# A planner's order table and its landing allowances replaced in a windowed-attention and expert-attention kernel

## The chip, the cores and the metric

One core of a Trainium2 chip runs the whole program. The metric is the device time of one execution in microseconds (us); the figure that counts is the median of several runs. TensorE is called PE here, VectorE DVE, ScalarE ACT, GpSimd POOL, and SP is the queue of SyncE, which issues nearly all DMAs.

## What is computed

Eight batches of 576 positions go through two layers. The first is attention in a window of 64 positions with 8 heads of 64; the second is four causal attentions ("experts"), of which a gate picks the best two for each position.

```python
# layer 1, for each batch and head
scores = scale * q @ k.T                      # 576 x 576, only 0 <= i - j < 64 is kept
attn = softmax(where(mask, scores, -1e9))
x = concat_heads(attn @ v)                    # 576 x 512
# layer 2, for each batch
logits = x @ w_gate                           # 4 experts, the best 2 are kept, softmax of the two
for e in range(4):
    q, k, v = x @ wq[e], x @ wk[e], x @ wv[e] # 576 x 64 each
    a = softmax(causal(scale * q @ k.T))
    out += weight_of_e * (a @ v @ wo[e])      # zero where e is not among the best two
```

## The kernel before

The code does not issue its instructions as it comes to them. `Plan` records them as operations (a run of matmuls that belongs together is one operation, everything else is one instruction), works out what depends on what, and then issues all of them in an order that it finds by playing the program through with its own costs. Four things set that order: the string `ORDER`, which gives PE's blocks one letter each and is obeyed strictly; due times on the other engines, worked back from the place that a block has in `ORDER` (`deadlines`); the table `EARLY`, which shifts the due time of single operations; and the costs that `Plan` assumes, one of which is `op["land"]` in `Plan.add`, the time from the end of a transfer's data to the moment when its reader may start. On the chip each engine then works its list off strictly from the top.

The letters of `ORDER`: s, t and a are layer 1 in 36 units of eight blocks of 64 positions: s the scores, t the transposes of the softmax, a the product with v. K, k, Q, q, V and W are the projections of layer 2 (k and q the second halves of a batch, W the last block of two batches), 1, 3, 2, 4 and 0 the score blocks of one *half*, A and B its products with v, O and o the output projection. A half is one batch and one pair of experts, so there are 16 of them, numbered 0 to 15 here. z is a pair of matmuls on the identity matrix whose result nobody reads; there are six. T and U are transposes on PE, in the last two halves only.

In halves 0 to 13 the probabilities are transposed without PE (`s2_t`): after the last score block, 4, the softmax is finished on DVE, ACT and POOL, DVE transposes 32x32 blocks into the buffer `ST` (`st` in the rows), and 16 DMAs on SP's queue move them to the buffer `PT2` (`pt`). These are the late moves inside SBUF that the title of the change speaks of; they are called the 16 moves below. `PT2` exists once: the 16 moves of a half wait for A and B of the half before. A and B both read all of it.

On the same queue of SP, in order, go the loads of layer 1 (`q`, `k` of 288 KB and `v` of 576 KB for each of 32 pairs of heads) and the stores of the result (`out`). Each of q, k and v has three buffers, so a load waits for the last s or a block that reads the buffer; a store waits for ACT's or DVE's copy out of PSUM. An instruction of SP that waits holds all behind it.

The weights come in f32 and are split by `split_weights` into two f32r parts (`wkhi`, `wklo` and so on); the result of layer 1 is split in the same way into `xh` (a copy on ACT) and `xl` (a subtraction on DVE) by `s1_av`. A projection block multiplies, for each of four pairs of heads in turn, xh, xl and xh again.

Of the kernel before, what the change touches and what calls it, by code (L numbers as in the profile page):

```python
# [31 lines left out]
OLATE = 1.7  # L32
TTAG = 1
ORDER = (
    "sszzsztstazazstKKVtssQaatQsVtastkqaatzss1tV2aaVt0s3s4WVqtVVkqQ132aV4s0tKQKtksaAa"
    "B132qta40kQtKsssAaBOO1324tqOV0VOtkKaaBAsstV132a0VQtkqaABass41tVWVOVOKOtqssa3240t"
    "OKOQkaBAatVk13240qtQQsssBaAaVtVOV13240VtOQsstOOqKqaBaAatKk13240qtkssaBAWVOVtOOQs"
    "s13240VKVtOOkaaAB1324tKQk0qssaaABtOO13s24tOO0KQktqBaAa13240VtVqVVaaABOWKOOQk1324"
    "0KOVqOQVBAVkKV13240QkqBAT1TOT23T4U0TUOTUOUTUOTAUBUooUoUoUoABOOOOO"
)  # L40
EARLY = {
# [52 lines left out]
}  # L94
HOLD = 13000.0
TAIL = 2
SHORT = 0
WARM = 6
TPE = 99
BPOS = 0.05  # L100
SJOIN = 1
PARTS = ((0, 5), (5, 9))
# [4 lines left out]
class Plan:  # L107
# [17 lines left out]
    def add(self, engine, call, name, out, args, kw):  # L125
        if engine == "P" and self.run is not None and self.run["engine"] == "P":
            op = self.run
# [7 lines left out]
        outs = [x for x in (out, kw.get("accum_out")) if x is not None]  # L135
# [8 lines left out]
                row = inner[0].nbytes() / inner[0].shape[0] / (inner[0].shape[1] if len(inner[0].shape) == 4 else 1)  # L144
                rows = inner[0].nbytes() / row
                op["transfer"] = outs[0].nbytes() / 420 + rows * (1.2 if row < 2048 else 0.4)
            op["land"] = 1650 if len(inner) == 2 else 2300 if outs[0].space == bass.MemoryType.SB else 500
        sb = [x for x in outs + ins if x.space != PSUM]
        op["port"] = engine == "G" or engine == "V" and (
            len([x for x in sb if x in ins]) > 1 or len(sb) == len(outs + ins) and name in (  # L150
# [1015 lines left out]
```

## Time and profile before

| | us |
|---|---|
| median of 3 runs | 424.93 (424.13 to 425.73) |
| the profiled execution | 423.19 |
| its span, first to last instruction | 421.5 |

| engine | busy, us | share of the span |
|---|---|---|
| PE | 404.1 | 96% |
| PE's weight loads | 364.4 | 86% |
| DVE | 310.3 | 74% |
| POOL | 276.2 | 66% |
| ACT | 269.6 | 64% |

The page's share of busy time for PE counts every matmul until its result has drained, so that neighbours overlap; what a block really takes is read from the start of one block to the start of the next, in the timeline. A row of the timeline gives the start from the beginning of the span, the length, engine and line, the operation, output and inputs, the shape, how many are merged, and in brackets an idle time ahead of it with what ended it. All recorded instructions carry one source line, so operations are told apart by their tiles.

### The profile page before, as it was taken

The page shows a single profiled execution, that of the slowest core. Times are in us where ns is not written, and L with a number is a line of the kernel's source. Part 1 is how long each engine was busy: PE and PEld are TensorE (multiplying, and loading weights), DVE is VectorE, ACT ScalarE, POOL GpSimd, SP SyncE. Part 2 cuts the span into 40 slices and gives each one's busy share as a digit, 9 for nine tenths or more (in the row PEclk, how much of TensorE's full clock was granted, in tenths as well). Part 3 has the DMA queues.
Part 4 walks back from the last instruction along what each step waited for, and adds up shares of the span by engine and source line. Part 5 has one row for each costly group of instructions (what it writes and reads, how often), then busy time and mean ns, then how long its engine had stood idle before and what let it go on. Part 6 is the DMA issues. An engine that isn't in the chain of part 4 may idle for free. (4 is left out here: it accounts for less than half of the span.)

```text
span 421.5 us, 13748 instructions
## 1 busy us (share of the span) xinstructions
PE 404.1 (96%) x5168; PEld 364.4 (86%) x5168; DVE 310.3 (74%) x997; ACT 269.6 (64%) x854; POOL 276.2 (66%) x473
## 2 busy tenths in 40 slices
PE   5799999999999999999699999999899999999995
PEld 4688989999899989899598998998889999998874
DVE  4899997879876876768677878679696756456722
ACT  3676685767685858566558566585567754727932
POOL 4778777697879687695687949567759553505310
PEclk9999999999999999999899999999999999999999
DMA  7979661467876572478776366369645623642113
GB/s 241 337 260 318 187 212 59 108 167 222 283 203 188 136 252 90 122 183 299 199 223 182 136 180 201 103 157 302 173 155 139 167 56 104 166 101 54 51 51 124
DMA packets 33361, 72.66 MB, mean 172 GB/s; under 512 B 6160, under 2 KB 10256, under 8 KB 33296
## 3 DMA queue, kind: packets, MB, share of 16 engines
q1 hardware_dynamic: 32640, 71.14, 56.6%
q8 instruction: 41, 0.67, 0.6%
q10 hardware_dynamic: 656, 0.66, 0.5%
q14 instruction: 24, 0.20, 0.1%
HBM read 39.85 MB, written 9.44 MB: 117 GB/s over the span
## 5 line engine op out<-in xcount | busy, mean ns | idle before, releaser
L381 POOL TENSOR_SCALAR_AFFINE_SELECT pt<-ft 64x512 f32<-64x512 f32 x126 | 83.6, 663 | 38.2 <-ACT ft L381 29.0
L381 POOL TENSOR_TENSOR sm<-sm,st 128x512 f32<-128x512 f32 x72 | 76.5, 1068 | 34.3 <-DVE st L381 24.2
L381 POOL TENSOR_SCALAR p<-p,r,g 128x320 f32<-128x320 f32 (+4 forms) x135 | 83.5, 633 | 11.9 <-DVE r L381 10.5
L381 PE MATMUL o<-pt,v 128*64 128x64 f32 (+2 forms) x1776 | 82.5, 250 | 6.3 <-DMA pt<-st 3.2
L381 ACT ACTIVATE p<-p,r 128x192 f32<-128x192 f32 (+4 forms) x135 | 77.9, 579 | 15.8 <-DVE r L381 15.5
L381 PEld LDWEIGHTS o<-pt,v 128*64 128x64 f32 x1776 | 69.7, 139 | 20.2 <-issue 7.4
L381 DVE STREAM_TRANSPOSE st<-p 128x128 f32<-128x128 f32 (+5 forms) x126 | 63.5, 521 | 19.0 <-POOL p L381 9.9
L381 DVE CUSTOM_DVE_ANT_0 p<-s,causal 128x320 f32<-128x320 f32 (+2 forms) x120 | 52.7, 482 | 3.7 <-PE s L381 3.3
L381 DVE TENSOR_REDUCE st<-sm 128x8 f32<-128x512 f32 x72 | 47.9, 674 | 5.6 <-ACT sm L381 5.0
L381 PE MATMUL s<-k,q 64*64 64x128 f32 (+1 forms) x1116 | 37.0, 277 | 5.3 <-DMA q<-in_qT_dram 5.0
L381 PE MATMUL s<-kt,qt 64*128 64x256 f32 (+2 forms) x480 | 41.9, 317 | 0.0
L381 PEld LDWEIGHTS s<-kt,qt 64*128 64x128 f32 x480 | 35.1, 185 | 4.4 <-issue 1.8
L381 PEld LDWEIGHTS s<-k,q 64*64 64x64 f32 x1116 | 30.9, 139 | 9.2 <-DMA k<-in_kT_dram 4.5
L381 PE MATMUL kps<-xh,wkhi 128*128 128x256 f32 (+1 forms) x128 | 38.8, 303 | 0.0
L381 PE MATMUL qps<-xh,wqhi 128*128 128x320 f32 (+1 forms) x128 | 38.6, 302 | 0.0
L381 PE MATMUL v2ps<-wvhi,xh 128*128 128x260 f32 x128 | 37.8, 296 | 0.0
L381 PE MATMUL qps<-xl,wqhi 128*128 128x320 f32 (+1 forms) x128 | 37.7, 294 | 0.0
L381 PE MATMUL qps<-xh,wqlo 128*128 128x320 f32 (+1 forms) x128 | 37.6, 294 | 0.0
L381 PE MATMUL kps<-xl,wkhi 128*128 128x256 f32 (+1 forms) x128 | 37.6, 294 | 0.0
L381 PE MATMUL kps<-xh,wklo 128*128 128x256 f32 (+1 forms) x128 | 37.6, 294 | 0.0
L381 PE MATMUL v2ps<-wvhi,xl 128*128 128x260 f32 x128 | 36.3, 284 | 0.0
L381 PE MATMUL v2ps<-wvlo,xh 128*128 128x260 f32 x128 | 36.2, 283 | 0.0
(125 smaller groups left out, 928.9 us busy)
## 6 DMA issues: line engine op xcount, KB each, us to landing
v<-in_vW_dram SPq DMA_DIRECT2D x28, 576.0 KB, 5.4
pt<-st SPq DMA_DIRECT2D x112, 116.0 KB, 2.3
pt<-st SPq DMA_DIRECT2D x112, 80.0 KB, 2.1
out_dram<-out SPq DMA_DIRECT2D x32, 256.0 KB, 2.2
q<-in_qT_dram SPq DMA_DIRECT2D x28, 288.0 KB, 4.5
k<-in_kT_dram SPq DMA_DIRECT2D x28, 288.0 KB, 4.9
v<-in_vW_dram SPq DMA_DIRECT2D x3, 320.0 KB, 8.3
out_dram<-out SPq DMA_DIRECT2D x7, 128.0 KB, 2.4
```

The costliest lines, as they stand in the source:

```text
L381: call(*args, **kw)
```

## The change

No operation is added, removed or resized. Three things are replaced: the string `ORDER` (the same letters, each as often as before, in another order), the table `EARLY`, and two allowances in `Plan.add`: a DMA from SBUF to SBUF is now assumed to land 2750 ns after its data instead of 1650, and a load 3000 ns instead of 2300. The allowances are used in planning alone; they put no wait into the program.

```diff
 ORDER = (
-    "sszzsztstazazstKKVtssQaatQsVtastkqaatzss1tV2aaVt0s3s4WVqtVVkqQ132aV4s0tKQKtksaAa"
+    "szszzsztstzaazstKVtKssaaQtVsQtastkaqtass1tV2aa30tVss4WVktQqVKV1Va324s0tQqktKaAsa"
...
-    "s13240VKVtOOkaaAB1324tKQk0qssaaABtOO13s24tOO0KQktqBaAa13240VtVqVVaaABOWKOOQk1324"
+    "13240OkVOVVtOaBA1324at0QqKsstkaABaK13tOOs240OqQtkOaABa3124q0VtVVVaaBAWOOKOkQK132"
...
 EARLY = {
-    0: 2100, 1: -1350, 2: 3350, 4: 5800, 5: 5300, 6: -8850, 7: 8050, 8: 72150, 9: 80300, 10: 5100,
+    3: -850, 4: 8900, 5: -7400, 6: -4000, 7: 13950, 8: 91150, 9: 75700, 10: 11400, 11: -4300, 12: 117550,
...
-            op["land"] = 1650 if len(inner) == 2 else 2300 if outs[0].space == bass.MemoryType.SB else 500
+            op["land"] = 2750 if len(inner) == 2 else 3000 if outs[0].space == bass.MemoryType.SB else 500
```

What that does at three places follows. The first is DVE's list in the opening, from the first half of the split of wv to the end of the split of layer 1's first two units (`o1_0` and `o1_1` are the results of units 0 and 1, `st1_3` belongs to the softmax of unit 3). Before:

```order
L381 SCALAR_TENSOR_TENSOR wvlo_173<-pt2_72,wvhi_172 128x4x256
L381 TENSOR_TENSOR xl0_121<-o1_0_119,xh0_120 128x2x256
L381 TENSOR_REDUCE st1_3_138<-sm1_3_137 128x8
L381 TENSOR_TENSOR xl0_121<-o1_1_131,xh0_120 128x2x256
L381 RECIPROCAL st1_3_138<-st1_3_138 128x8
L381 SCALAR_TENSOR_TENSOR wvlo_173<-pt2_72,wvhi_172 128x4x4
```

Now:

```order
L382 SCALAR_TENSOR_TENSOR wvlo_173<-pt2_72,wvhi_172 128x4x256
L382 TENSOR_REDUCE st1_3_138<-sm1_3_137 128x8
L382 TENSOR_TENSOR xl0_121<-o1_1_131,xh0_120 128x2x256
L382 RECIPROCAL st1_3_138<-st1_3_138 128x8
L382 SCALAR_TENSOR_TENSOR wvlo_173<-pt2_72,wvhi_172 128x4x4
L382 TENSOR_TENSOR xl0_121<-o1_0_119,xh0_120 128x2x256
```

The subtraction for unit 0 has gone from the first place behind the split to the last.

The second is SP's queue ahead of the moves of half 5, which begin with the last row (`q22` to `v21` are loads for pairs of heads 19 to 23, `out_1_2` and `out_1_3` results of batch 1). Before:

```order
L381 DMA v19_499<-in_vW_dram 128x1152
L381 DMA out_0_dram<-out_1_3_480 128x512
L381 DMA out_0_dram<-out_1_2_482 128x512
L381 DMA q22_493<-in_qT_dram 128x576
L381 DMA k22_494<-in_kT_dram 128x576
L381 DMA q23_538<-in_qT_dram 128x576
L381 DMA k23_539<-in_kT_dram 128x576
L381 DMA v20_547<-in_vW_dram 128x1152
L381 DMA v21_549<-in_vW_dram 128x1152
L381 DMA pt2_72<-st2_71 32x640 x2
```

Now:

```order
L382 DMA q22_493<-in_qT_dram 128x576
L382 DMA k22_494<-in_kT_dram 128x576
L382 DMA q23_538<-in_qT_dram 128x576
L382 DMA k23_539<-in_kT_dram 128x576
L382 DMA out_0_dram<-out_1_2_482 128x512
L382 DMA v19_499<-in_vW_dram 128x1152
L382 DMA v20_547<-in_vW_dram 128x1152
L382 DMA pt2_72<-st2_71 32x640
```

The four loads of q and k stand ahead of the store, one store fewer is among them, and v21 has gone behind the moves.

The third is the same queue ahead of the moves of half 7. Before:

```order
L381 DMA q27_643<-in_qT_dram 128x576
L381 DMA k27_644<-in_kT_dram 128x576
L381 DMA out_0_dram<-out_2_3_582 128x512
L381 DMA out_0_dram<-out_2_2_584 128x512
L381 DMA v24_600<-in_vW_dram 128x1152
L381 DMA v25_652<-in_vW_dram 128x1152
L381 DMA pt2_72<-st2_71 32x928 x2
```

Now:

```order
L382 DMA out_0_dram<-out_2_2_584 128x512
L382 DMA q27_643<-in_qT_dram 128x576
L382 DMA k27_644<-in_kT_dram 128x576
L382 DMA q28_649<-in_qT_dram 128x576
L382 DMA k28_650<-in_kT_dram 128x576
L382 DMA v24_600<-in_vW_dram 128x1152
L382 DMA v25_652<-in_vW_dram 128x1152
L382 DMA pt2_72<-st2_71 32x640 x2
```

Six loads in a row now stand directly ahead of these moves, where there were two.

## Rows read from the trace of the kernel before

**Rows 1.** The page: busy time of the engines.
```profile
PE 404.1 (96%) x5168; PEld 364.4 (86%) x5168; DVE 310.3 (74%) x997; ACT 269.6 (64%) x854; POOL 276.2 (66%) x473
```

**Rows 2.** PE's waits, longest first: us in total, times, longest us.
```profile
PE s L381 <- DMA q<-in_qT_dram: 5.0, 3, 4.5
PE o L381 <- DMA pt<-st: 3.2, 1, 3.2
PE o L381 <- issue: 1.3, 1, 1.3
PE o L381 <- POOL pt L381: 1.2, 2, 0.9
```

**Rows 3.** Timeline of PE around the products of half 5 (o).
```profile
201.39 0.31 PE L381 MATMUL qps<-xl,wqhi 128*128 128x320 f32 x1
201.54 0.31 PE L381 MATMUL qps<-xh,wqlo 128*128 128x320 f32 x1
201.78 2.75 PE L381 MATMUL s<-k,q 64*64 64x128 f32 x96
207.70 6.01 PE L381 MATMUL o<-pt,v 128*64 128x256 f32 x104 [3.17 <-DMA pt<-st]
```

**Rows 4.** Timeline of SP ahead of the moves of half 5: the first load, the moves.
```profile
186.13 0.49 SPq L381 DMA_DIRECT2D q<-in_qT_dram  x1
...
191.34 14.64 SPq L381 DMA_DIRECT2D pt<-st  x16
```

**Rows 5.** DMA issues, KB each and us to landing: 191 to 195 us; the whole span.
```profile
pt<-st SPq DMA_DIRECT2D x3, 116.0 KB, 6.6
...
pt<-st SPq DMA_DIRECT2D x112, 116.0 KB, 2.3
```

**Rows 6.** Windows of 1 us: PE, PEld, DVE, ACT, POOL busy, granted clock, DMA share, GB/s.
```profile
206.00:207.00 1.00, 0.00 (x0) 0.00 (x0) 0.00 (x0) 0.00 (x0) 0.00 (x0) 0.98 0.84 196
209.00:210.00 1.00, 1.00 (x8) 0.69 (x6) 0.96 (x3) 0.63 (x1) 1.00 (x3) 0.50 1.07 398
210.00:211.00 1.00, 1.00 (x24) 0.84 (x22) 1.00 (x3) 0.00 (x0) 1.00 (x3) 0.82 1.07 364
```

**Rows 7.** Timeline in half 9: the first load on SP, the products on PE.
```profile
282.09 0.53 SPq L381 DMA_DIRECT2D q<-in_qT_dram  x1
...
304.04 1.83 PE L381 MATMUL o<-pt,v 128*64 128x256 f32 x25 [1.30 <-issue]
```

**Rows 8.** Timeline in half 11: its last scores on PE, its moves on SP.
```profile
312.78 1.23 PE L381 MATMUL s<-kt,qt 64*128 64x448 f32 x12
...
328.26 11.33 SPq L381 DMA_DIRECT2D pt<-st  x16
```

**Rows 9.** Timeline of DVE in the opening.
```profile
22.69 0.69 DVE L381 TENSOR_TENSOR xl<-o,xh 128x512 fp32r<-128x512 f32 x1
23.30 0.68 DVE L381 TENSOR_REDUCE st<-sm 128x8 f32<-128x512 f32 x1
23.89 0.68 DVE L381 TENSOR_TENSOR xl<-o,xh 128x512 fp32r<-128x512 f32 x1
24.49 0.19 DVE L381 RECIPROCAL st<-st 128x8 f32<-128x8 f32 x1
...
24.64 1.22 DVE L381 SCALAR_TENSOR_TENSOR wqlo<-pt,wqhi 128x1024 fp32r<-128x1024 f32 x1
```

**Rows 10.** Timeline of PE in the opening, and where one stall ended later.
```profile
24.23 0.28 PE L381 MATMUL kps<-xl,wkhi 128*128 128x256 f32 x1
...
39.60 0.66 PE L381 MATMUL t<-ident,sm 128*128 128x128 f32 x4 [0.44 <-POOL sm L381]
...
48.92 0.61 PE L381 MATMUL warm<-ident 128*128 128x128 f32 x4
49.46 0.78 PE L381 MATMUL s<-k,q 64*64 64x64 f32 x22
...
291.64 0.63 PE L381 MATMUL t<-ident,sm 128*128 128x128 f32 x4 [0.56 <-DVE r L381]
```

More of the change, by code (lines that the diff above doesn't have):

```diff
@@ L34 @@
 ORDER = (
-    "sszzsztstazazstKKVtssQaatQsVtastkqaatzss1tV2aaVt0s3s4WVqtVVkqQ132aV4s0tKQKtksaAa"
-    "B132qta40kQtKsssAaBOO1324tqOV0VOtkKaaBAsstV132a0VQtkqaABass41tVWVOVOKOtqssa3240t"
-    "OKOQkaBAatVk13240qtQQsssBaAaVtVOV13240VtOQsstOOqKqaBaAatKk13240qtkssaBAWVOVtOOQs"
-    "s13240VKVtOOkaaAB1324tKQk0qssaaABtOO13s24tOO0KQktqBaAa13240VtVqVVaaABOWKOOQk1324"
-    "0KOVqOQVBAVkKV13240QkqBAT1TOT23T4U0TUOTUOUTUOTAUBUooUoUoUoABOOOOO"
+    "szszzsztstzaazstKVtKssaaQtVsQtastkaqtass1tV2aa30tVss4WVktQqVKV1Va324s0tQqktKaAsa"
+    "B132a0tkQq4sstKsAaBOqO13240OtVkVOtVVssaABatK132aatQ0qkssBaA14tVOWOKOOtVss324t0Vq"
+    "QVkOqaBaA1324atK0QktKsssaAaBQOtO13240OktOVQtVsssAaaBKVqtq1324t0VkaaBAWOqQsstKVOs"
+    "13240OkVOVVtOaBA1324at0QqKsstkaABaK13tOOs240OqQtkOaABa3124q0VtVVVaaBAWOOKOkQK132"
+    "40QkKOOqBA13240VVVVQkq1ABTOTOT3T4U2U0TUOUTOUTATBUoUoUoUoUoABOOOOO"
 )
 EARLY = {
[52 rows of a table removed]
[53 rows of a table added]
 }
```

103 rows, old and new, of the table EARLY are left out of this document.

## The prediction

> **What bounds the kernel now.** I read the page first: PE is busy for 404.1 of 421.5 us, the next engine, DVE, for 310.3 [rows 1]. So the order of PE's blocks is the time, plus every moment in which PE waits. The second view is therefore PE's list of waits [rows 2]: 5.0 us go on the first loads, which no order of blocks can shorten, 3.2 us on one wait for the 16 moves, 1.3 us on another idle time, and stalls of at most 0.9 us follow. The timeline then shows where each lies.
>
> The 3.2 us are one stall: scores of layer 1 start at 201.78, and the products of half 5 at 207.70, after 3.17 us idle for the moves [rows 3]. It cost more than that. The granted clock, 0.98 in the microsecond before 207, is 0.50 after it (1.2 instead of 2.4 GHz), and 0.82 from 210 to 211, so back at full speed from about 210.4 [rows 6]. From 207.70 to 210.4 PE worked at half speed: 1.3 us lost. The second stall, 1.30 us, stands before the products of half 9 at 304.04 [rows 7].
>
> Why the moves were late is on SP. In half 5 six loads leave from 186.13 on, and the moves start at 191.34 and take 14.64 us to be issued [rows 4], where half 11, with one load just ahead, takes 11.33 [rows 8]. The 116 KB moves issued from 191 to 195 land after 6.6 us, against 2.3 in the median [rows 5]. So the moves queue behind loads issued just ahead of them.
>
> **The change part by part.** The sum is made against the profiled execution (423.19 us, the span of 421.5 and 1.7 around it) and carried over to the median of 424.93, which lies 1.7 above that execution.
>
> *Changes of shape on PE.* A block of another shape starts later behind its predecessor than one of the same shape: 0.24 us from the last projection matmul at 201.54 to the scores at 201.78, against 0.15 within the block [rows 3]. Counting the letters of `ORDER`, neighbours of different shape rise from 198 to 202. With the gap of each kind of pair read from the timeline like this one, the 384 gaps grow by **0.3 us** in all; bounds 0.1 and 1.0 (four times 0.24). The Trainium skill (TensorEngine Tiling, Key Properties) says that changing the tiling mode drains the engine, and so speaks against an order with more changes; it names no price there, and four whole gaps would make the sum 0.7 worse.
>
> *The stalls that go.* In half 5 the four loads of q and k now stand ahead of the store that held them, so they can leave when their buffers come free and not together with the loads of v; v21 goes behind the moves. I laid out both orders by the distances from block to block that the timeline shows where PE does not stall. By that the last load, v20, is released 15.3 us after the half's last scores, and the products come at 31.5. 16 moves at 0.71 us (11.33/16 [rows 8]) and 2.3 us to land [rows 5] need 13.6, so 2.6 us remain: its 3.2 + 1.3 us go. In half 9 one load of v comes late, 11.9 us after the scores, and the products come at 28.9: 11.9 + 13.6 leaves 3.4, and the 1.3 us go too. Together **-5.8 us**.
>
> *New stalls of the same kind.* By the same distances two halves look short. In half 7 six loads in a row now stand ahead of the moves. In half 5 it took 21.6 us from the first of six such loads to the products (186.13 to 207.70 [rows 3, 4]), in half 9 22.0 (282.09 to 304.04 [rows 7]); the new order leaves 20.6 between the block that frees the first of them and the products of half 7. 1.0 to 1.4 us are missing; I take 1.0. In half 11 one K block (12 matmuls 0.147 us apart [rows 3]) and one transpose block fewer stand in between, so PE comes for the data 25.8 us after the last scores instead of 27.7. Those scores ended at 314.0, the moves began 14.3 us later and took 11.33 to issue [rows 8]. If the softmax is no quicker now, 1.9 us are missing; if it is ready when the products of half 10 end, none. I take 1.0, all other halves at zero. The lower bound of this term is 0; the upper is that no half gets from its scores to its last move faster than it did, which sums to 4.6 us (halves 4, 7, 9 and 11 short by 0.5, 1.0, 1.3 and 1.8). **+2.0 us.**
>
> *The opening.* One of six z blocks leaves 48.92, where PE has real work next (0.54 us until 49.46 [rows 10]), for the opening, where PE waits for data anyway: -0.5. Against that, DVE's subtraction for unit 0 now stands behind a reduction (0.59 from start to start), the other subtraction (0.61), a reciprocal and the small split (0.15 together): it starts at 24.04 instead of 22.69 and ends at 24.73 [rows 9]. The first K block reads it in its second matmul, at 24.23 before [rows 10]: 0.6 later (bounds 0 and 1.0, since ACT's changed list can add 0.4). A stall behind it, transposes at 39.60 that waited for POOL (0.44, some 0.6 between the blocks [rows 10]), is then swallowed, since POOL's list up to there is almost the same and PE comes later: -0.6. Sum **-0.5 us**, bounds -1.1 and +0.5.
>
> *The stall at 291.64*, transposes directly behind scores that waited for DVE (0.56 [rows 10]), has a product block of layer 1 in front of it now: **-0.6**. The other small stalls I leave as they are; a new order can double them or do without, 1.5 us either way.
>
> The sum is 0.3 - 5.8 + 2.0 - 0.5 - 0.6 = -4.6 us. From 424.93 that is 420.3 us (418.6 for an execution like the profiled one).
>
> **The rivals.** *The moves come late again.* If the new stalls reach their upper bound, 4.6, the gain is 2.0 and the time 422.9, and with the opening at its worst 423.9. For it speaks that longer allowances by themselves make nothing faster, and that half 5 came 3.17 us late though the old plan had meant it to fit; against it, that its loads are no longer bunched. The Trainium skill (DMA: Bandwidth & Descriptors, Queues, rings and completion order) says that each DMA engine consumes descriptors in ring order, by which loads issued just ahead of the moves always go first. The 6.6 us of rows 5 agree.
>
> *All of these stalls go.* Then their term is 0, and without K's wait as well the time is 424.93 - 4.6 - 2.0 - 0.6 = 417.7. The allowance for the moves grew by 1.1 us and half 9 was short by 1.3, so this nearly covers it; against it stand the six loads of half 7.
>
> *Slower: a store holds the loads.* In half 5 the loads of q and k were issued some 13 us after the blocks that free their buffers, because two stores stood ahead of them. Now a store stands ahead of loads in halves 3, 5, 7, 8 and 9. If ACT makes the copies for these stores so late that the loads of two halves are 3 us late or more, each costs what half 5 did, 3.2 + 1.3 = 4.5. Two of them in place of my 2.0 give 420.3 - 2.0 + 9.0 = 427.3. It decides from a store that leaves some 5 us or more behind its block on PE.
>
> **How the numbers follow.** A measurement of this kernel can tell a difference of about 0.5%, 2.1 us, from none: below 422.8 is faster, above 427.1 slower. My forecast (new stalls of 1 to 4 us, 418.5 to 422.8) has 0.52, the late moves again (422.8 to 425.5) 0.24, all stalls gone (416.5 to 418.5) 0.14, the held loads 0.10. Faster is 0.52 + 0.14 = 0.66, same 0.24, slower 0.10. The range, 417.0 to 425.5, reaches from the case without these stalls, less part of the small ones, to the late moves with the opening at its worst and 1.5 us of small stalls more. The predicted time is 420.3.
>
> **What would show it.** In the profile after: no idle time of 3 us before the products of half 5, and the granted clock at 1.00 there; about 1 us before the products of halves 7 and 11; the moves of half 7 issued in more than 12 us, those of half 5 in about 11; a gap inside the first K block between 24 and 25 us; no transposes waiting for DVE right behind scores near 290. I am wrong if PE waits for moves in halves where I gave none, if POOL or DVE turns up as what PE waits for (I compared distances on PE, not all of their lists), or if a long idle time takes the clock down again.

## The result and the profile after

The changed kernel takes 420.26 us in the median of its runs (419.15 to 422.05); the kernel before took 424.69 in the same comparison. The ratio is 0.990 (0.986 to 0.994). Measured once more, in the rounds of the last experiments on the opening, it is 0.993 (0.991 to 0.995): 419.71 against 422.96. So the gain lies between 3 and 4.4 us. The profiled execution takes 420.33 us, 2.9 less than that of before, with a span of 418.6.

First PE's waits, as in [rows 2]: what PE waited for, the total in us, how often, and the longest one.

```profile
PE s L382 <- DMA k<-in_kT_dram: 5.4, 2, 4.4
PE o L382 <- POOL pt L382: 2.3, 3, 1.8
PE t L382 <- POOL sm L382: 1.3, 4, 0.6
PE o L382 <- DVE r L382: 0.8, 2, 0.6
PE o L382 <- issue: 0.4, 1, 0.4
```

The 3.2 us for the moves are gone, and so is the place where the clock had fallen. But 2.3 us for POOL's `pt` stand where 1.2 stood, and the first loads cost 5.4 us instead of 5.0. Half 5, first SP's rows and then PE's (start, length, operation, shape, count; an idle time ahead would stand in brackets):

```profile
184.30 0.53 SPq L382 DMA_DIRECT2D q<-in_qT_dram  x1
...
188.09 2.42 SPq L382 DMA_DIRECT2D v<-in_vW_dram  x2
191.96 10.60 SPq L382 DMA_DIRECT2D pt<-st  x16
202.66 0.53 SPq L382 DMA_DIRECT2D v<-in_vW_dram  x1
```

```profile
203.53 2.75 PE L382 MATMUL s<-k,q 64*64 64x128 f32 x96
206.21 2.04 PE L382 MATMUL o<-pt,v 128*64 128x64 f32 x48
```

Against [rows 3] and [rows 4]: the moves start no earlier (191.96; 191.34 before), but are issued in 10.60 us instead of 14.64, since v21 (202.66) comes behind them. The last one lands at 204.0, and the products, which the row of 206.21 holds behind a block of layer 1, follow at 207.2 without a wait. The granted clock, with the columns of [rows 6], is at full speed there; it fell in another place:

```profile
23.00:24.00 1.00, 1.00 (x5) 0.78 (x5) 1.00 (x2) 1.00 (x3) 0.77 (x1) 0.50 1.02 377
207.00:208.00 1.00, 1.00 (x30) 0.86 (x26) 1.00 (x4) 0.38 (x1) 1.00 (x2) 1.00 0.97 348
210.00:211.00 1.00, 1.00 (x17) 0.91 (x14) 1.00 (x2) 1.00 (x3) 1.00 (x2) 1.00 1.06 394
```

SP's moves of half 7, and then PE at the products of halves 7, 9 and 11:

```profile
236.64 10.80 SPq L382 DMA_DIRECT2D pt<-st  x16
```

```profile
249.79 3.48 PE L382 MATMUL o<-pt,v 128*64 128x64 f32 x72
...
300.99 1.22 PE L382 MATMUL o<-pt,v 128*64 128x256 f32 x20 [0.38 <-issue]
...
337.80 3.53 PE L382 MATMUL o<-pt,v 128*64 128x64 f32 x74
```

The products of halves 7 and 11 (inside the rows of 249.79 and 337.80) follow the blocks ahead of them without a wait; half 9 keeps 0.38 of its 1.30 [rows 7]. The loss is in the opening. These rows answer to [rows 9, 10]:

```profile
6.53 1.13 PE L382 MATMUL s<-k,q 64*64 64x64 f32 x16 [1.05 <-DMA k<-in_kT_dram]
7.59 1.22 PE L382 MATMUL warm<-ident 128*128 128x128 f32 x4
8.74 0.92 PE L382 MATMUL s<-k,q 64*64 64x64 f32 x14
...
21.22 0.45 PE L382 MATMUL o<-pt,v 128*64 128x64 f32 x8 [1.76 <-POOL pt L382]
...
22.84 1.23 PE L382 MATMUL warm<-ident 128*128 128x128 f32 x4
...
26.60 0.28 PE L382 MATMUL kps<-xl,wkhi 128*128 128x256 f32 x1
```

Unit 0's second pair of heads starts after 1.05 us idle for k (6.53; it was 5.84), then a block z takes 1.15 us in front of unit 1's scores (8.74; it was 7.24), unit 1's products come at 21.22 instead of 19.71, and K's second matmul at 26.60 instead of 24.23.

### The profile page after: what moved, and what is told of

Same layout as the page of the kernel before. It is cut to its first block, busy times and chain, and to the rows that moved or that the text cites. A ratio compares the mean times of both kernels' runs of the same rounds, so it can differ in the third digit from the quotient of the medians.

```text
span 418.6 us, 13752 instructions
## 1 busy us (share of the span) xinstructions
PE 403.8 (96%) x5168; PEld 363.7 (87%) x5168; DVE 313.1 (75%) x997; ACT 268.7 (64%) x854; POOL 274.9 (66%) x473
## 4 chain that ended last, share of the span: by engine, by line
PE 81%; DVE 9%; POOL 5%; issue 2%; DMA 1%; ACT 1%; ACTq 0%; POOLq 0%; DVEq 0%
PE o L382 17%; PE s L382 15%; PE qps L382 11%; PE kps L382 11%; PE ops L382 11%; PE v2ps L382 11%; PE t L382 5%; DVE st L382 3%; POOL sm L382 2%; DVE p L382 2%; DVE sm L382 2%; POOL pt L382 1%; DVE pt L382 1%; POOL p L382 1%; DMA k<-in_kT_dram 1%
## 5 line engine op out<-in xcount | busy, mean ns | idle before, releaser
L382 POOL TENSOR_SCALAR p<-p,r,g 128x320 f32<-128x320 f32 (+3 forms) x135 | 83.4, 632 | 13.0 <-DVE r L382 11.4
L382 ACT ACTIVATE p<-p,r 128x320 f32<-128x320 f32 (+4 forms) x135 | 77.7, 578 | 15.1 <-DVE r L382 14.5
L382 PE MATMUL o<-pt,v 128*64 128x64 f32 (+2 forms) x1776 | 80.8, 248 | 3.7 <-POOL pt L382 2.3
L382 DVE COPY_PREDICATED sm<-own,s 128x256 f32<-128x256 uint8 x72 | 29.3, 437 | 13.0 <-ACT sm L382 10.4
L382 PE MATMUL kps<-xh,wkhi 128*128 128x320 f32 (+1 forms) x128 | 38.9, 304 | 0.0
L382 PE MATMUL qps<-xh,wqhi 128*128 128x256 f32 (+1 forms) x128 | 38.9, 304 | 0.0
L382 PE MATMUL qps<-xh,wqlo 128*128 128x256 f32 (+1 forms) x128 | 37.7, 294 | 0.0
L382 PE MATMUL kps<-xh,wklo 128*128 128x320 f32 (+1 forms) x128 | 37.7, 294 | 0.0
L382 PE MATMUL kps<-xl,wkhi 128*128 128x320 f32 (+1 forms) x128 | 37.7, 294 | 0.0
L382 PE MATMUL qps<-xl,wqhi 128*128 128x256 f32 (+1 forms) x128 | 37.6, 294 | 0.0
```

The source lines that it names most:

```text
L382: call(*args, **kw)
```

## Experiments on the opening

In all experiments that move rows, the list of instructions that the plan had found was kept and only the rows named were put elsewhere, so every other row stands where it stood. The changed kernel's ACT list begins with k of unit 1. The first run puts it back, the second moves the z block, the third does both:

```diff
 ACT's first rows (k_76 and k_78 are unit 0's, k_80 is unit 1's)
-DMA k_80<-in_kT_dram
 DMA k_76<-in_kT_dram
 DMA k_78<-in_kT_dram
+DMA k_80<-in_kT_dram
```

```diff
 PE's first blocks
 s (unit 0)
-z
 s (unit 1)
+z
 z z
```

> The kernel after, with one row moved: ACT's load of k for unit 1 (k_80) goes back behind the two loads of unit 0 (k_76, k_78), as in the kernel before. All other lists stay as they are. Theory (the opening lost its time to the order of the first loads and to the z block): in the kernel after the second pair of unit 0 starts at 6.53 us after 1.05 us idle for k, against 5.84 before, so it starts about 0.7 us earlier here, and what follows to the first K block with it: -0.7 us, 419.6 for a median of 420.3. Rival (POOL's list is what sets the opening, the loads are covered by it): the products of unit 1 stay at 21.2 us and the time at 420.3 within 0.3.

> The kernel after, with one block moved: the z block (four matmuls on the identity) that stands between the scores of units 0 and 1 goes behind the scores of unit 1, where one stood before too. Theory (the z block was not free): it takes 7.59 to 8.74 us, so the scores of unit 1 start 1.15 us earlier, POOL's part of the softmax with them, and the products of unit 1 come at about 20.1 instead of 21.22: -1.1 us, and some -0.5 to -0.9 more in executions where the granted clock fell to 0.5 after the idle time of 1.76 us ahead of those products: 419.0 for a median of 420.3. Rival (PE waits for POOL there anyway, the z block hides): the scores of unit 1 are earlier but the products stay at 21.2, the time at 420.3 within 0.3.

> The kernel after with both: the loads of k of unit 0 ahead of that of unit 1, and the z block behind the scores of unit 1. Theory: the scores of unit 1 start at about 7.2 us as before instead of 8.74, the products of unit 1 at about 19.7 instead of 21.22, no fall of the clock behind them; K's second matmul then waits for the split xl, which POOL and PE do not move (it ended at 26.23), unless DVE's list comes earlier too: between -0.6 (K held by DVE) and -2.4 (all of it): I take -1.7, 418.6 for a median of 420.3. Rival (what is gained here is waited for later, at the loads and small waits between 40 and 75 us): 420.3 within 0.5.

The table gives these and the later ones beside the changed kernel; each time stands against the kernel before in the same rounds. The last column is the start of PE's last block in the trace, against the changed kernel's 413.7. The two traces of the changed kernel itself end 1.1 us apart, while their rows of the opening agree within 0.2 us; so what a run did to the opening is read from those rows, not from the end.

| kernel | median, us | ratio to before | last block, us |
|---|---|---|---|
| changed kernel, first and second time | 420.26, 419.71 | 0.990 (0.986 to 0.994), 0.993 (0.991 to 0.995) | 0, +1.1 |
| k of unit 0 first | 418.28 | 0.989 (0.985 to 0.992) | -1.9 |
| z behind unit 1's scores | 418.06 | 0.988 (0.984 to 0.992) | +1.2 |
| both | 418.84 | 0.990 (0.986 to 0.993) | -0.8 |
| both, and xl first on DVE | 419.09 | 0.990 (0.987 to 0.994) | -0.6 |

The loads alone did what was expected and a little more: unit 0's scores ran through, z stood at 6.35 instead of 7.59, and the whole opening came 1.2 us earlier. With the z block behind unit 1's scores, the products of unit 1 came at 20.49 instead of 21.22 (20.1 had been expected), and PE met a new wait in K's second matmul. Both together were expected at 418.6 and ran at 418.84. First the run with k alone, then that with z alone, then that with both:

```profile
6.35 1.22 PE L382 MATMUL warm<-ident 128*128 128x128 f32 x4
```

```profile
27.08 0.58 PE L382 MATMUL kps<-xl,wkhi 128*128 128x256 f32 x1 [1.27 <-DVE xl L382]
```

```profile
26.20 0.39 PE L382 MATMUL kps<-xl,wkhi 128*128 128x256 f32 x1 [1.33 <-DVE xl L382]
```

1.27 and 1.33 us for the split `xl`: the wait that the prediction had put at 0.6 and that the kernel after does not show, because there PE is late by more. So two chains lead to K side by side, PE's scores with POOL, and DVE's splits, and each covers the other. The z block's expectation (-1.1 us) missed in its trace, which is that of its slowest execution (421.55 us): the clock fell in that wait and stood at 0.50 until 33.2. Its median, 418.06, is no worse for it:

```profile
26.00:27.00 1.00, 0.00 (x0) 0.00 (x0) 1.00 (x5) 1.00 (x5) 0.54 (x1) 0.70 1.04 384
...
32.00:33.00 1.00, 1.00 (x7) 1.00 (x6) 0.52 (x1) 0.00 (x0) 0.00 (x0) 0.50 0.00 0
34.00:35.00 1.00, 1.00 (x19) 0.86 (x21) 0.97 (x3) 0.63 (x4) 0.91 (x2) 1.00 0.03 8
```


Then DVE's subtraction went back too, and the changed kernel itself ran beside it:

```diff
 DVE
 SCALAR_TENSOR_TENSOR wvlo<-pt,wvhi 128x4x256
+TENSOR_TENSOR xl<-o_0,xh
 TENSOR_REDUCE st_3<-sm_3
 TENSOR_TENSOR xl<-o_1,xh
 RECIPROCAL st_3<-st_3
 SCALAR_TENSOR_TENSOR wvlo<-pt,wvhi 128x4x4
-TENSOR_TENSOR xl<-o_0,xh
```

> The kernel after with its opening undone on three engines: ACT's loads of k and the z block as in the run with both of these, and on DVE the subtraction xl of unit 0 directly behind the large split of wv, as in the kernel before. Theory (with loads and z block put back, the opening is held by DVE alone: K's second matmul waited 1.33 us for that subtraction and started at 26.20): it starts at about 24.7 to 25.0 us here, 1.2 to 1.5 earlier than in the run without this row and 1.6 to 1.9 earlier than in the kernel after, and the end of the program with it: some 1.3 us less than the run without this row, 2.1 less than the kernel after, so 417.0 to 418.5. Rival (DVE is late as a whole, because its split of wv took 2.1 us there against 1.17 before, so another of its rows takes the place of this one): K starts at 25.8 or later and 0.5 us or less is won.

> The kernel after, unchanged, on the same chip and in the same rounds as the two kernels beside it, so that they have a base. Both theories: its ratio to the kernel before as measured first, 0.9897 (0.986 to 0.994); in the trace the opening as in the first profile (products of unit 1 at 21.2 us, K's second matmul at 26.6) and no wait for the moves in half 5.

```profile
24.32 0.38 PE L382 MATMUL kps<-xl,wkhi 128*128 128x256 f32 x1
...
40.70 0.66 PE L382 MATMUL t<-ident,sm 128*128 128x128 f32 x4 [1.08 <-POOL sm L382]
```

K's second matmul starts at 24.32, earlier than expected, and 2.3 us earlier than in the kernel after. But little of that is kept: the transposes at 40.70 wait 1.08 us for POOL's `sm`, the stall of [rows 10] (39.60) come back. They stand at 41.43 in the kernel after, so 2.3 us won at K are 0.7 at 41 us, and 0.6 us at the end. Against the changed kernel in the same rounds the time fell by 0.6 us, not by the 2.1 expected.

The times don't show what the opening cost the change: the four kernels with parts of it undone have ratios of 0.988 to 0.990, the changed kernel 0.993 and 0.990, and the intervals overlap. The rows show it up to 41 us. The first K block starts 1.2 us earlier with k first, 1.9 with both and 2.4 with `xl` too, and of these 1.2, 0.6 and 0.7 are left at the transposes of 41.43; most of what DVE's row wins is given back at the wait for POOL.

## Experiments on half 5

The prediction said that the moves queue behind loads issued just ahead, and that the change cures this in two ways: the loads of q and k leave earlier, and v21 goes behind the moves. Both ways were put into the kernel before, then v21 alone; and in the kernel after, the loads of q and k were held back behind the store and v19.

```diff
 SP in the kernel before; the second run moves v21 alone
 DMA v19
+DMA q22, k22, q23, k23
 DMA out_1_3, out_1_2
-DMA q22, k22, q23, k23
 DMA v20
-DMA v21
 DMA pt<-st x16
+DMA v21
```

```diff
 SP in the kernel after
-DMA q22, k22, q23, k23
 DMA out_1_2
 DMA v19
+DMA q22, k22, q23, k23
 DMA v20
 DMA pt<-st x16
 DMA v21
```

> The kernel before, with SP's list changed at half 5 alone: the four loads of q and k stand ahead of the two stores, and the load v21 behind the 16 moves, as in the kernel after. PE's and all other lists stay. Theory (the moves of half 5 were late because six loads left just ahead of them): the moves are issued in 10 to 12 us instead of 14.64, the 3.2 us ahead of the products go and with them the 1.3 us at half clock: 424.7 - 4.5 = 420.2. Rival 1 (the stall hid a later one, so the gain is given back at halves 6 to 9): 422 to 424. Rival 2 (the loads of half 6, v21 among them, become late): a wait of 1 us or more ahead of a block of layer 1 at 208 to 215 us, 422 to 424.

> The kernel before with one row moved on SP: the load v21 (576 KB) goes behind the 16 moves of half 5; the four loads of q and k stay behind the two stores. Theory (bytes of loads just ahead of the moves make them late): 1.7 MB stand ahead instead of 2.3 MB, the moves start 0.5 us earlier and take about 12.6 instead of 14.64 us: 2.5 of the 3.2 us go, and the fall of the clock with them: -2.5 to -3.8, 421 to 422.2. Rival (that the loads of q and k are held by the stores is what matters): the stall keeps at least 2 us, -0.5 to -1.2, 423.5 to 424.2.

> The kernel after with SP's list changed at half 5 alone: the four loads of q and k stand behind the store and the load v19, just ahead of v20 and the moves, so that they wait with the store and all leave together. Theory (loads issued just ahead make the moves late): the loads leave between about 189 and 192 us, the moves start at about 193.3 instead of 191.96 and take some 14 instead of 10.6 us: 4.7 us later, against the 3.2 they had to spare: a stall of 1.5 us ahead of the products of half 5 and a fall of the clock of up to 1.3: +1.5 to +2.8, 421.8 to 423.1 for a median of 420.3. Rival (the load v21 behind the moves was what mattered, the place of q and k does nothing): the moves take 10 to 11 us, no stall, 420.3 within 0.3.

| kernel | median, us | ratio to before | 16 moves issued, us | last one landed | products of half 5 |
|---|---|---|---|---|---|
| before | 423.4 in the rounds of the first two | 1 | 14.64 from 191.34 | 207.50 | 207.70 |
| before, q and k early, v21 behind | 421.49 | 0.995 (0.992 to 0.998) | 13.94 from 191.45 | 206.85 | 206.98 |
| before, v21 behind | 419.31 | 0.992 (0.989 to 0.995) | 11.53 from 190.69 | 205.37 | 205.51 |
| before, v20 and v21 behind | 421.00 | 0.993 (0.990 to 0.996) | 11.10 from 191.28 | 205.86 | 206.10 |
| after | 420.26 | 0.990 (0.986 to 0.994) | 10.60 from 191.96 | 204.03 | 207.19 |
| after, q and k held back | 420.59 | 0.995 (0.993 to 0.997) | 12.17 from 191.80 | 207.28 | 207.42 |

One load moved, v21, gives 0.8% (3.3 us by the ratio, 4.1 by the medians; 2.5 to 3.8 were expected), where the whole change gives 0.7 to 1.0%. In its trace the last block starts 4.2 us earlier, and 3.0 of these arise at half 5; 0.6 arise at half 9, where nothing had been moved. With q and k early as well it was 1.9 us instead of 4.5, and 2.52 of the 3.17 us of stall stayed, so that they leave early won nothing here. The moves start at 190.7 to 192.0 us in all six, since they wait for DVE's transposes, not for the queue. Held back, q and k did make the moves of the kernel after later, by 3.2 us at the last landing: the last move was issued 1.4 us later (203.38 instead of 201.97) and took 3.91 us to land instead of 2.06, which is the subject of the next section. That used up the spare, and PE waited 0.34 us at the products; the ratio of 0.995 can't be told from the changed kernel's 0.993. What SP waited for between 187.5 and 206, in the run with both and in that with v21 alone:

```profile
SPq L381 <- DVE st L381: 3.0, 1, 3.0
SPq L381 <- DMA v<-in_vW_dram: 2.1, 1, 2.1
```

```profile
SPq L381 <- DVE st L381: 2.3, 1, 2.3
...
SPq L381 <- DMA v<-in_vW_dram: 0.8, 1, 0.8
```

The second row of each had been overlooked, and the kernel before has it too, with 2.3 us: a move waits for the *landing* of a load. Which one, the times tell. In the kernel before, the load v21 is issued at 189.6 and takes 9.4 us to land, so until 199.0; the eighth move leaves at 199.04. With v21 alone moved, the last load ahead is v20, issued at 188.0 and landed 8.6 us later, at 196.6; the eighth move leaves at 196.62. The first pair of fences is the kernel before, the second the run with v21 moved (the load alone with its time to landing, then the eighth and ninth move):

```profile
L381 SPq DMA_DIRECT2D v<-in_vW_dram x1: 377/377/377, 189.6 to 189.6; - x1
...
DMA to landing us min/median/max: 9.4/9.4/9.4
```

```profile
199.04 1.14 SPq L381 DMA_DIRECT2D pt<-st  x2
```

```profile
L381 SPq DMA_DIRECT2D v<-in_vW_dram x1: 382/382/382, 188.0 to 188.0; - x1
...
DMA to landing us min/median/max: 8.6/8.6/8.6
```

```profile
196.62 1.14 SPq L381 DMA_DIRECT2D pt<-st  x2
```

In the two other kernels with a load of v last it is the same (landed 198.60, eighth move 198.67; 198.31 and 198.38). The program gives SP's transfers eight semaphores in turn, and each transfer waits until the one before it on its semaphore has landed; `Plan.order` counts with the same eight (`LANES`). So seven moves can leave behind the loads and the eighth waits for the last of them.

That gave a forecast of its own: with v20 behind the moves too, the last load ahead lands before the eighth move is due.

```diff
 SP, kernel before
 DMA q22, k22, q23, k23
-DMA v20, v21
 DMA pt<-st x16
+DMA v20, v21
```

> The kernel before with both loads of v (v20, v21) behind the 16 moves of half 5, and nothing else moved. In the run with v21 alone moved, the eighth move left at 196.62 us, 0.06 after v20 had landed (196.56), and PE still waited 1.81 us. Theory (a move waits until the eighth transfer ahead of it has landed, so it is the last load ahead of the moves that counts): now the last load ahead is k23, which landed at 192.96 there, before the eighth move is due; the moves leave without a gap in about 10 us from 190.7, the last lands at about 203, and the wait ahead of the products is 0.5 us or less: 1.3 to 1.8 us less than with v21 alone, 417.5 to 418.2 at the median. Rival (the softmax on DVE sets it): the moves start at 190.7 as before and the wait stays at 1.5 to 1.8 us, 419.3. Second rival: v20, first used 1.8 us behind the products, comes too late and PE waits for it instead, 419 to 420.

The moves did leave without that gap, 11.10 us from 191.28, and SP's waits show no load any more. But PE still waited 1.56 us ahead of the products, and the median was 421.00, not 417.5 to 418.2. The profile puts this wait down to a load of v, as the second rival had it; but v20 landed at 207.07, when the products had begun (206.10), so they did not wait for it. The last move, issued at 201.78, landed only at 205.86, 4.1 us later, where its neighbours took 2.1 to 2.3. In the run with v21 alone the last two took 4.2 and 3.7. This was the new question. (Besides, this trace loses 1.50 us at half 9, where the one with v21 alone loses 0.27.)

## What held the last moves

Queue 8 is named "instruction" in the profile's account of the queues; it moves 41 packets of 16 KB in an execution (its row on the page of the kernel after: packets, MB, share of the engines' time):

```profile
q8 instruction: 41, 0.67, 0.7%
```

In the run with v21 alone one of them begins at 202.25, while the last two moves are under way. Counted in the records of all thirteen profiles at hand by then, with the moves left out that had a load or a store in flight ahead of them: 913 moves had no packet of an instruction queue beginning from 2 us before their issue to 2.2 us after it, and landed after 2.1 us in the median and 2.4 at most. In 257 cases a packet of queue 8 began 0.8 to 2.1 us after a move's issue, and in all but five of them that move or the one behind it took 3.1 to 4.4. The Trainium skill (Advanced Engine Details and Errata, Sequencer and Instruction Queues) gives a line of the instruction cache as 16 KB or 256 instructions; the trace agrees, with 10,336 matmuls and weight loads [rows 1] in 41 packets, 252 each. In the five kernels with PE's old list (one of them, with the new allowances alone, comes below) the 22nd packet begins when PE has started 5,484 to 5,549 of these records. So the packet has its place in PE's code, and should move when the code ahead of it is lengthened:

```diff
 PE, kernel before with v21 moved
+MATMUL warm<-ident 128x64 x10
 MATMUL s_0_0<-k_76,q_75 64x64 x2
```

> The run with v21 alone moved behind the moves of half 5, and ten matmuls on the identity (128 by 64 columns, each counted twice by the profile, with as many weight loads: 40 records of PE) put at PE's start, where it waits 4.3 us for its first loads. Nothing else moves; the result of the ten is read by nobody. In the run without them the last two moves of half 5 (issued at 200.99 and 201.62 us) landed after 4.2 and 3.7 us instead of 2.1 to 2.3, and PE waited 1.81 us; a 16 KB packet of the queue that fetches instructions began at 202.25, when PE had started 5628 of its records (at some 24 in a microsecond there). Theory (such a packet holds up the moves in flight): the packet belongs to a place in PE's code, so it comes 40 records or 1.7 us earlier in the program's course; it meets moves that leave 1.3 to 2 us before the last, the last ones land after 2.1 to 2.5 us, and the wait ahead of the products of half 5 is 0.7 us or less. Time: 1.1 to 1.8 us less than without, and up to 1.0 more where the added matmuls outlast the first loads: 417.5 to 419.3 at the median against 419.3. Rival (the last moves of a half are slow by themselves, by their rows or by other traffic there): they land after 3.7 us or more again and the wait stays at 1.5 to 1.9 us.

The first two fences are the run without the ten matmuls: the stretch of 0.2 us in which the packet begins (packets, MB, share of the engines), and the last move's time to landing. The others are the run with them: the packet, the moves of 200.56 and of 204.47, and PE at the products.

```profile
q8 instruction: 1, 0.02, 53.9%
```

```profile
  PE o L381: 1.8, 1
...
DMA to landing us min/median/max: 3.7/3.7/3.7
```

```profile
q8 instruction: 1, 0.02, 35.4%
```

```profile
DMA to landing us min/median/max: 2.1/2.8/3.4
```

```profile
DMA to landing us min/median/max: 2.1/2.2/2.3
```

```profile
203.80 2.75 PE L381 MATMUL s<-k,q 64*64 64x128 f32 x96
206.67 4.83 PE L381 MATMUL o<-pt,v 128*64 128x256 f32 x108
```

The packet came at 201.66, 4.9 us ahead of the last landing instead of 3.1, and met the moves issued at 200.56, 201.20 and 201.83 (3.4, 3.1 and 2.8 us); the last three took 2.3, 2.3 and 2.1, and the products at 206.67 followed the scores without a wait. The rival is out. The packet moved by more than planned: it began when PE had started 5,419 of its records, the 40 included, where the same count as without them, 5,508, had been expected. Why, these runs don't tell. The program as a whole won less: 418.75 us, ratio 0.990 (0.987 to 0.993), within the interval of the run without. PE waited elsewhere instead: the ten matmuls outlast the first loads by 1.7 us, most of which comes back at the next loads, but then PE waited 1.36 and 1.44 us for POOL in the opening, where the clock fell, 0.99 for a load of v at 42.50 and 0.71 for DVE at 122.17.

Half 9 is the same thing once more. Its last move took 3.9 us before (issued 299.92, a packet at 301.15), and in the kernel after again 4.1 (issued 296.76, a packet at 297.98). With 2.2 us it would have landed at 302.1 before, ahead of the 302.74 at which PE began to wait, and the 1.30 us of [rows 7] would not be there. This was not run. The other traces with PE's old list lose 0.27 to 1.50 us at this place, and in each of them a packet begins near the last moves.

## The allowances and the table apart

```diff
 the kernel before with its old table; the second run does the reverse in the kernel after
-op["land"] = 1650 if len(inner) == 2 else 2300 if ...
+op["land"] = 2750 if len(inner) == 2 else 3000 if ...
```

> The kernel before with the two allowances alone (2750 ns for a DMA inside SBUF, 3000 ns for a load), the old table. PE's list is the same; on SP no load passes a move and half 5 keeps its six loads ahead of its moves; DVE's, ACT's and POOL's lists change in many places. Theory (the allowances alone take nothing away): the stall of 3.2 us stays, 424.7 within 1.5. Rival (the allowances carry the gain): the stall of half 5 is gone, 420 to 421.

> The kernel after with the old allowances (1650 and 2300 ns) and the new table. PE's list is the same; on SP v21 stays behind the moves of half 5, two loads go ahead of the moves of half 4; DVE's, ACT's and POOL's lists change in many places, in the opening too. Theory (the table was fitted to its allowances): half 5 keeps its gain, but lists that were not fitted cost small stalls: 420.3 + 1 to 4, 421 to 424. Rival (the allowances do nothing, the table carries all): 420.3 within 1.

The allowances alone cost 0.4% (424.36 us, ratio 1.004, 1.001 to 1.007); the new table with the old allowances costs 1.1% (427.66 us, 1.011, 1.008 to 1.015), more than expected. PE's waits in the first and in the second:

```profile
PE o L381 <- DMA pt<-st: 3.0, 1, 3.0
PE t L381 <- POOL sm L381: 2.5, 3, 1.0
```

```profile
PE t L382 <- POOL sm L382: 3.8, 4, 2.2
PE kps L382 <- DVE xl L382: 1.7, 1, 1.7
```

With the old table the stall of half 5 stays, 3.0 us; with the new one it is gone under either allowance, but DVE, ACT and POOL get an order in which PE waits, most of all in the opening (1.7 us for `xl`, and 2.2 of the 3.8 for POOL). So neither half of the change is a gain by itself: the table carries the cure of half 5, and it was fitted to its allowances.

## Why the prediction was right and where it was wrong

The time came out as forecast, 420.3, but that was luck in part. By the second measurement, 0.993 of 424.93, it would be 421.9, and the sum 1.6 us too good; and the sum was made against the profiled execution, which got 2.9 us faster and not 4.6. With what the rows show in the place of each term it is 0.3 - 4.5 - 0.9 + 0 + 2.3 + 0 = -2.8: the two terms that were furthest off, by 2.0 and 2.8 us, were wrong in opposite directions.

**Half 5: right, for half of its reason.** 3.2 us of stall and 1.3 at half speed went, as written. Bunched loads did make the moves late. That q and k "can leave when their buffers come free" brings the moves of the kernel after 1.4 us forward, which its spare covers, and won nothing in the kernel before; v21 did it, through the eighth move's wait for the last load's landing. And part of the old stall was the code packet at 202.75: the move issued at 201.50 took 4.0 us to land and that of 202.78 took 1.94 us to issue instead of 0.6. The spare of 2.6 us that I had worked out was 3.2, but with luck: the code packet came at 206.38, behind the last landing. In the run with k first and in that with both changes of the opening one met the last move of half 5 (3.67 and 3.71 us to landing), and no spare was left.

**Half 9: mostly the wrong reason.** I laid 1.3 us to a late load; 0.9 went. The load did hold the eighth move (landed 294.85, move at 294.91), but for some 0.4 us only; what made the last move late, by 1.8 us before and 2.0 after, was a code packet.

**New stalls, +2.0: the step that failed first.** Nothing was late in halves 7 and 11. For half 7 I had priced six loads in a row by the 21.6 and 22.0 us that halves 5 and 9 took from the first load to the products. But the moves are not tied to the first load: they started at 236.64, behind DVE's transposes (done at 236.58) and the products of the half before (236.60), and the last load had landed (241.07) before the eighth move was due (241.79), so they were issued in 10.80 us, not in over 12. In half 11 the moves began 12.0 us after the last scores instead of 14.3 (325.84 and 328.26), the case that the prediction named for a price of zero.

**The opening, -0.5: the step that failed worst.** The first scores of half 0 and of half 2 have the same blocks ahead of them in both orders, so their starts can be compared as they are (two rows before, two after):

```profile
51.27 0.39 PE L381 MATMUL s<-kt,qt 64*128 64x256 f32 x2
...
95.80 0.38 PE L381 MATMUL s<-kt,qt 64*128 64x256 f32 x2
```

```profile
53.24 0.39 PE L382 MATMUL s<-kt,qt 64*128 64x256 f32 x2
...
98.09 0.39 PE L382 MATMUL s<-kt,qt 64*128 64x256 f32 x2
```

So the term was +2.0 at half 0 and +2.3 by half 2; 0.6 of it came back by the first output block (116.16 instead of 114.44). I had counted z as free because "PE waits for data anyway", and looked at DVE's list, not at the head of ACT's, where k of unit 1 went ahead of unit 0's. The z block did not hide: it stood between two scores that had their data. It moved POOL's whole chain by as much, and the clock fell for 3.4 us behind the wait of 1.76 us that grew there. The 0.6 us for `xl` was in the right place, but covered; uncovered it was 1.3. The stall at 39.60 was swallowed, as written, and returned as soon as PE came earlier.

**The stall at 291.64** went, and DVE's `r` is waited for one block earlier instead, 0.58 us ahead of the product block at 288.84, so the -0.6 was not won. **Changes of shape** (+0.3) can't be told from the rest.

Of the rivals, "all of these stalls go" was right on halves 7 and 11, and its 417.7 would have been near had the opening cost nothing: the kernels with the opening mended ran at 418.1 to 419.1. The held loads did not happen. Two of the three signs that I had named for being wrong were there, POOL among PE's waits and a fallen clock, both in the opening. The Trainium skill (DMA: Bandwidth & Descriptors, Queues, rings and completion order) says that each engine consumes descriptors in ring order, though a later one may finish before an earlier one. The landings agree with the first: they follow the order of issue among all the loads and moves of half 5 (from 189.40 to 207.50 in the kernel before). The wait that cost the time was another, at the program's own semaphores.

## What to carry to other kernels

Where transfers share a fixed number of semaphores, a short move is held until the long load that many places ahead of it has landed, so it is the last load in front of a burst of moves that has to go, not the loads in general. A filler block that is free between two waits is not free between two blocks that have their data; look at what stands on both sides, and at every engine's list of the opening. And a gain ahead of an engine that is nearly late (POOL here) can be given back at the next place where it is waited for, so such edits are to be priced at the end of the chain and not where they stand.

## What was not expected of the hardware

A 16 KB packet of PE's instruction queue holds up the small moves in flight beside it by 1 to 2 us (3.1 to 4.4 us to landing instead of 2.1); there are 41 of them in an execution; where it meets the last move before a block that needs them all, PE waits, and lengthening PE's code by 40 records moved it away, further than by these 40.

The fall of the clock did not go by the length of a wait alone. It fell to 0.50 (1.2 GHz) behind a wait of 1.76 us ahead of unit 1's products, and behind one of 1.44 us at the same place in the run with the ten matmuls; in the run with v21 moved, PE waited 1.81 us ahead of the products of half 5, and the microsecond behind it had the full 2.4 GHz:

```profile
206.00:207.00 1.00, 1.00 (x16) 0.83 (x14) 1.00 (x4) 0.00 (x0) 0.63 (x1) 1.00 0.95 373
```

What makes the difference these runs don't tell. They also leave open why one 256 KB store took 2.5 us to land behind its neighbour, and held v20 until 198.60, in the run with q and k early; a packet of queue 8 began 0.3 us after the store ahead of it had landed, but that one was not moved.
